# Attention and MoE on one core: seven products instead of eight for three quarters of the first pair's hidden layer

## Chip, core and metric

The kernel runs on one core of one Trainium2 chip. The metric is device time in microseconds (us), lower is better. Engines are named as the profile names them: PE (TensorE), PEld (its weight loads), ACT (ScalarE), DVE (VectorE), POOL (GpSimd) and SP (SyncE, which only issues transfers here).

## What is computed

Sigmoid attention over 8 batches, 12 heads, 448 positions and 64 channels, then a gated two-layer network over all 3584 tokens:

```
scores = q @ k^T / sqrt(64) - log(448)
attn   = sigmoid(scores)
x      = attn @ v              # heads side by side: 3584 x 768
h      = x @ w_in              # 3584 x 2048
g      = h * sigmoid(h)
out    = g @ w_out             # 3584 x 768
```

The kernel holds q, k, v and the weights as float16, accumulates in float32 and returns float32.

## The kernel before

The eight batches are taken in four pairs m = 0 to 3. For attention a *group* g is four heads of one batch (24 groups, three to a batch), and each group has seven *units* (g, ch), one per 64-row chunk of keys for two head pairs.

**Attention.** `scores` (L209) makes one unit: eight quarter-array products, four at a time, into one of two double PSUM banks (`psc`), then one ACT sigmoid of 128x896 (L223). Two units make a *burst* (`burst`, L722). `values` (L231) multiplies the seven units of a group with v: 28 quarter-array products into two banks `pav`, which DVE scales into `xT` (L256). Work of the second layer kind is put between the bursts so that PE has something to do while ACT makes sigmoids. PE takes its instructions strictly in the order of the program, and so do ACT and DVE; a helper of the language puts in the waits between engines.

**Hidden layer, pairs 1 to 3.** `h_pair` (L348) computes a pair's h with Strassen-Winograd's seven block products in place of eight: the tokens of the two batches are the block rows of x, the two halves of w_in's rows and columns are its blocks. For each of eight column groups i there are seven products `m1` to `m7` of three 128x128x448 matmuls each (21 in place of 24). They need four sums over w_in (`w_in_sums`, L308: tiles `SI1`, `SI2`, `SI4`, and one sum in place), made once for all pairs, and four sums over x (`x_sums`, L334: tiles `tx` 1, 2, 4, and one in place in `xT`), made per pair. The products are put together by five DVE additions of 128x448 per column group (`plus`, L374).

**Hidden layer, pair 0.** `first_h` (L537) uses no such sums: `h_unit(b, fc)` (L273) is six matmuls of 128x128x448 for one batch b and one of 16 column blocks fc, so 192 in all. For batch 0 the result is evicted by an ACT sigmoid into a room of the tag `tx` and a DVE multiplication (L291, L292), since ACT's loaded table is the sigmoid's while bursts run. For batch 1 ACT's Silu is used (L296). Four matmuls each of the first two units are issued early (`begin`, L676). Then batch 1's bursts (units n = 24, 26, ... 40) alternate with stretches of the stream: `stretch(stream, 1600)` (L712) takes matmuls, at 189 ns each, until 1600 ns are due, that is eight or nine. What is left of the 192, 99 matmuls, runs as one dense stretch after the bursts (L743). During this the sums over w_in (12 of 16 DVE instructions, the rest comes in the first out set) and over w_out (`w_sums`, L452: `T2`, `T3`, `T4` and one in place, 14 of 16, on DVE) are made, and `dma_transpose` (L198) prepares the k and q of groups 6, 7 and 8: a DVE copy of 128x896 (L202) and a transposing transfer by SP.

**Output layer.** `out_set` (L473) does two row blocks with seven products of eight 128x128x384 matmuls each, with the sums `T2` to `T4` over w_out and DVE sums over `gTr`. `sets` (L556) runs three or four of them per pair; after 14 matmuls of the first set the next pair's bursts are put among them.

**PSUM banks.** During bursts four single banks serve everything but `psc` (`one_bank`, L84). `banks_for_h` (L74) makes all eight single, in a ring that starts at the single bank that it takes for the oldest. A new tile in a bank waits until the old one's last reader is done.

```
    stream = first_h()
    stretch(stream, 1600)
    for n in range(NT_B + 3, 2 * NT_B, 2):
        burst(n)
        if n in (26, 30):
            transposes(5, "k" if n == 26 else "q")
        stretch(stream, 1600)
    values_if_any()
    for _ in stream:
        pass
```

Of the kernel before, what the change touches and what calls it, by code (L numbers as in the profile page):

```python
# [2 lines left out]

# [14 lines left out]
def kernel(  # L18
# [14 lines left out]
    P = 128  # L33
# [238 lines left out]

    def h_unit(b, fc):  # L273
        ph = one_bank("ph")
        for at, cc in enumerate(pairs):
            assert b in ready or at < 4
            nc.tensor.matmul(  # L277
                ph[:, :S],
                w_in_sb[:, cc, fc * P : (fc + 1) * P],
                xT[b][:, cc, :],  # L280
                start=(at == 0),
                stop=(at == NCC - 1),
            )
            if at < NCC - 1:
                yield 189
        if fc == NFC - 1:
            h_done.add(b)
        to = gTr[:, fc, first_col(0) + b * S : first_col(0) + (b + 1) * S]
        if b == 0:
            tsig = room_x()[:, 0]  # L290
            nc.scalar.activation(tsig, ph[:, :S], AF.Sigmoid, bias=0.0, scale=ISX)  # L291
            nc.vector.scalar_tensor_tensor(  # L292
                out=to, in0=ph[:, :S], scalar=ISX, in1=tsig, op0=ALU.mult, op1=ALU.mult
            )
        else:
            nc.scalar.activation(to, ph[:, :S], AF.Silu, bias=0.0, scale=ISX)  # L296
        yield 189


# [8 lines left out]
    def w_in_sums():  # L308
        for i in (1, 2, 4):
            si[i] = cpool.tile([P, NQ, NH], F16, tag=f"SI{i}", name=f"SI{i}")  # L310
        quarter = NH // 4

        def piece(at, op, o, x, y):
            cols = slice(at * quarter, (at + 1) * quarter)
            op(o[:, :, cols], x[:, :, cols], y[:, :, cols])

        add, sub = nc.vector.tensor_add, nc.vector.tensor_sub
        for half in range(2):
            for at in (2 * half, 2 * half + 1):
                piece(at, add, si[1], wi[1][0], wi[1][1])  # L320
                yield
            for at in (2 * half, 2 * half + 1):
                piece(at, sub, si[2], si[1], wi[0][0])
                yield
        for at in range(4):
            piece(at, sub, si[4], wi[0][1], si[2])
            yield
        for at in range(4):
            piece(at, sub, si[3], wi[0][0], wi[1][0])
            yield  # L330
# [3 lines left out]
    def x_sums(m, lo, hi):  # L334
        if lo == 0:
            for i in (1, 2, 4):
                tx[m, i] = room_x()
        of = slice(lo, hi)
        x0, x1 = ([xT[2 * m + j][:, c * NQ : (c + 1) * NQ] for c in range(2)] for j in range(2))
        sub = nc.vector.tensor_sub  # L340
        sub(tx[m, 1][:, of], x1[0][:, of], x0[0][:, of])
        sub(tx[m, 2][:, of], x1[1][:, of], tx[m, 1][:, of])
        sub(x1[0][:, of], x1[1][:, of], x1[0][:, of])
        sub(tx[m, 4][:, of], x0[1][:, of], tx[m, 2][:, of])

    NG = NFC // 2

    def h_pair(m, last_values):  # L348

        x0, x1 = xT[2 * m], xT[2 * m + 1]  # L350
# [11 lines left out]
        def product(i, to, w, x, start=True):  # L362
            for n in range(NQ):
                nc.tensor.matmul(  # L364
                    to,
                    w[:, n, i * P : (i + 1) * P],
                    x[:, n],
                    start=(start and n == 0),
                    skip_group_check=not start,
                    stop=(n == NQ - 1),  # L370
                )

# [25 lines left out]
        def m7(i):  # L398
            bank[i, "c"] = one_bank("pc")[:, :S]
            product(i, bank[i, "c"], si[3], x1[:, :NQ])  # L400
            got[i, "u3"], got[i, 22] = scratch(), scratch()
            plus(got[i, "u3"], bank[i, "c"], got[i, "u2"])
# [9 lines left out]
        def m3(i):  # L412
            product(i, bank[i, "d"], si[4], x1[:, NQ:], start=False)
            plus(bank[i, "d"], bank[i, "d"], got[i, "u2"])
            silu(i, 0, 1, bank[i, "d"])
# [3 lines left out]

        last = NG - 1  # L420
        order = [(m1, 0), (m1, 1), (last_values,), (m1, 2)]
        for i in range(3):
            order += [(m2, i), (silu11, i)]
        order += [(m5, 0), (m6, 0), (m7, 0), (h22, 0), (m1, 3)]
        for i in range(last):
            if i > 0:
                order += [(m7, i), (m5, i), (h22, i)]
            if 3 < i + 2 <= last:
                order += [(m1, i + 2)]
            order += [(silu22, i), (m6, i + 1)]  # L430
            if i < last - 1:
                order += [(m4, i), (m3, i)]
            if 2 < i + 2 < last:
                order += [(m2, i + 2), (silu11, i + 2)]
        order += [(m7, last), (m5, last), (h22, last), (m2, last), (silu11, last)]
        order += [(silu22, last), (m4, last - 1), (m3, last - 1), (m4, last), (m3, last)]
# [3 lines left out]
        h_done.update((2 * m, 2 * m + 1))  # L440

# [10 lines left out]
    def w_sums():  # L452
        for i in (2, 3, 4):
            tw[i] = cpool.tile([P, NHC, NO2], F16, tag=f"T{i}", name=f"T{i}")
        tw[1] = wq[0][1]
        for o, x, y in (
            (tw[3], wq[1][1], wq[0][1]),
            (tw[1], wq[0][1], wq[0][0]),
            (tw[2], wq[1][1], tw[1]),
            (tw[4], tw[2], wq[1][0]),  # L460
        ):
            for f in range(0, NHC, 2):
                nc.vector.tensor_sub(o[:, f : f + 2], x[:, f : f + 2], y[:, f : f + 2])
                yield
# [8 lines left out]
    def out_set(a1, rows1, a2, rows2, last=False):  # L473
# [13 lines left out]
        def product(a, w):  # L487
            po = one_bank("po")
            for fc in range(NHC):
                nc.tensor.matmul(  # L490
                    po[:, :NO2], a[:, fc, :], w[:, fc, :], start=(fc == 0), stop=(fc == NHC - 1)
                )
                if fc < NHC - 1:
                    yield 163
            return po[:, :NO2]
# [6 lines left out]
        yield 163  # L502
# [5 lines left out]
        yield 163  # L508
# [3 lines left out]
        yield 163  # L512
        po = yield from product(sg[2], tw[3])
        add(c22, po, c12)
        yield 163
        po = yield from product(a2[:, hi], tw[4])
        sub(c21, c22, po)
        yield 163
# [4 lines left out]
        yield 163  # L523
# [6 lines left out]
        yield 163  # L530

    by_h1 = {3: 6, 6: 7, 9: 8}
    early = [h_unit(0, fc) for fc in range(2)]
    sums = w_sums()
    in_sums = w_in_sums()

    def first_h():  # L537
        for b in range(2):
            for fc in range(NFC):
                yield from early[fc] if b == 0 and fc < 2 else h_unit(b, fc)  # L540
                if b == 0 and fc >= 10 or b == 1 and fc < 6:
                    next(in_sums)
                if b == 0:
                    continue
                if fc >= 2:
                    next(sums)
                if fc in by_h1:
                    for name in ("k", "q"):
                        dma_transpose(by_h1[fc], name, nc.vector.tensor_copy)
                    if by_h1[fc] == 8:  # L550

                        nc.gpsimd.tensor_copy(gate, qkT["q", 8][:1, 0, :1])
                        for to in (9, 10, 11):
                            load("kq", to)

    def sets(m):  # L556
        for g in range(0, NCH - 1, 2):
# [3 lines left out]
            for i, ns in enumerate(step):  # L561
                if m == 0 and g == 0 and i in (10, 14):
                    next(sums)
                if m == 0 and g == 0 and i in (20, 28, 36, 44):
                    next(in_sums)
                yield ns
# [62 lines left out]
    def after_values(g):  # L629
# [16 lines left out]
        if g >= 2 * NQ and g % (2 * NQ) == 2 * NQ - 2:  # L646
# [63 lines left out]
    done = due = 0.0  # L710

    def stretch(stream, ns, spent=0):  # L712
        nonlocal done, due
        due += ns
        done += spent
        while done < due:
            step_ns = next(stream, None)
            if step_ns is None:
                return
            done += step_ns  # L720

# [13 lines left out]
    stream = first_h()  # L735
    stretch(stream, 1600)
    for n in range(NT_B + 3, 2 * NT_B, 2):
# [3 lines left out]
        stretch(stream, 1600)  # L741
    values_if_any()
    for _ in stream:  # L743
        pass

    ENDING, FIRST_DENSE = 8, 14
    for m in range(B // 2 - 1):
        if m > 0:
            banks_for_attention()
# [20 lines left out]
        nc.scalar.activation(warm, bias_s, AF.Silu)  # L770
# [3 lines left out]
        waiting.clear()  # L774
        banks_for_h()
        values(g, NCH - 1)

        def last_values():
            values(g)
            after_values(g)  # L780
            x_sums(m + 1, NQ - 1, NQ)
            nc.gpsimd.tensor_copy(gate, tx[m + 1, 4][:1, NQ - 1, :1])

        for i, _ in enumerate(h_pair(m + 1, last_values)):
# [35 lines left out]
```

## Time and profile before

| what | value |
|---|---|
| median of 3 runs | 375.65 us (375.52 to 375.68) |
| the profiled execution's own time | 375.68 us |
| its span, first to last instruction | 373.7 us |
| granted TensorE clock over the span | 0.998 |
| PE busy | 363.9 us, 97% of the span |
| DVE, ACT, POOL busy | 252.2, 251.3, 77.4 us |

The first pair by stages, from the trace's timeline (us from the span's start):

| stage | from | to |
|---|---|---|
| start, batch 0's units up to 23 | 0 | 27.78 |
| first stretch, then batch 1's bursts n = 24 to 40 with 8 or 9 matmuls behind each | 27.78 | 55.58 |
| values of group 5 | 55.58 | 57.08 |
| dense stretch, 99 matmuls | 57.08 | 75.85 |
| out sets of pair 0 with the bursts of batches 2 and 3 begin | 75.85 | |

A row of the timeline is: start, time, engine, line, operation, output <- input, shapes, how many; in square brackets the idle time of the engine before it and what ended it. Times of several instructions in one row run from the first's start to the last's end; PE's rows overlap, because matmuls are pipelined and each one's shown duration (353 ns) is longer than the distance to the next.

### The profile page before, as it was taken

Reading aid. Unit: us, or ns where it says so; the run is one execution under the profiler, and the core shown is the slowest. Engines: PE = TensorE matmul, PEld = TensorE weight load, DVE = VectorE, ACT = ScalarE, POOL = GpSimd, SP = SyncE. Lnnn points to the kernel's source line nnn. Section 1 sums busy time; section 2 is a strip of 40 time slices with the busy share of each in tenths; the row PEclk is TensorE's granted clock in tenths of the full one; section 3 lists DMA queues with packets and bytes.
Section 4 is the critical chain, followed back from the end, with each engine's and each line's share of the span. In section 5 each row is a group of like instructions: output and inputs, shape, how many; then the busy total and the mean of one; then the engine's idle time right before and its main releaser. Section 6 shows DMA issues by size and latency. Waiting matters only on the chain.

```text
span 373.7 us, 7596 instructions
## 1 busy us (share of the span) xinstructions
PE 363.9 (97%) x3009; PEld 182.4 (49%) x3009; DVE 252.2 (67%) x458; ACT 251.3 (67%) x339; POOL 77.4 (21%) x116
## 2 busy tenths in 40 slices
PE   7999999999999999999999999999999999999995
PEld 3554445544444455544444545544444545555553
DVE  2565469867655687867575758795655768797763
ACT  5998885479888756687777846679888946650000
POOL 8566521040051072000014046000100000000000
PEclk9999999999999999999999999999999999999999
DMA  8999999996769599008579669921964030003333
GB/s 133 201 204 204 204 204 204 166 142 128 124 107 210 117 129 172 18 0 128 107 137 165 142 129 134 109 37 28 171 97 97 2 87 0 3 0 84 86 84 84
DMA packets 65698, 42.78 MB, mean 114 GB/s; under 512 B 36096, under 2 KB 62208, under 8 KB 65664
## 3 DMA queue, kind: packets, MB, share of 16 engines
q0 software_dynamic: 27072, 22.58, 42.3%
q1 hardware_dynamic: 38240, 19.44, 27.1%
q8 instruction: 23, 0.38, 0.4%
q10 hardware_dynamic: 352, 0.30, 0.2%
q14 instruction: 11, 0.09, 0.1%
HBM read 45.61 MB, written 11.01 MB: 152 GB/s over the span
## 4 chain that ended last, share of the span: by engine, by line
PE 79%; DMA 9%; ACT 6%; issue 2%; DVE 2%; POOL 0%; ACTq 0%
PE po L490 31%; PE psc L216 9%; PE pa L364 7%; PE pav L245 7%; PE pc L364 7%; PE pd L364 7%; ACT attnT L223 5%; PE ph L277 5%; DMA kf<-in_k_dram 5%; PE pb L364 4%; DMA qf<-in_q_dram 2%; DMA w_in_sb<-in_moe_w_in_dram 2%; PE pw L174 2%; ACT gTr L358 1%; PE ptrq L187 1%
## 5 line engine op out<-in xcount | busy, mean ns | idle before, releaser
L223 ACT ACTIVATE attnT<-psc,bias_s 128x896 f16<-128x896 f32 x168 | 159.2, 1009 | 25.9 <-PE psc L216 25.5
L490 PEld LDWEIGHTS <-S 128*128 128x128 f16 x448 | 40.8, 98 | 36.3 <-issue 10.0
L216 PE MATMUL psc<-qT,kT 64*64 64x448 f16 x672 | 54.8, 364 | 3.0 <-ACT attnT L223 1.8
L256 DVE TENSOR_SCALAR xT<-pav 128x448 f16<-128x448 f32 x48 | 27.7, 620 | 32.5 <-PE pav L245 32.5
L115 POOL DMA_DIRECT2D vf<-in_v_dram x24 | 17.2, 716 | 135.6 <-PE pav L245 131.4
L490 PEld LDWEIGHTS <-gTr 128*128 128x128 f16 x336 | 30.8, 98 | 27.7 <-issue 9.7
L490 PE MATMUL po<-w_out_sb,gTr 128*128 128x384 f16 x224 | 42.5, 327 | 0.1
L490 PE MATMUL po<-T,S 128*128 128x384 f16 x224 | 42.5, 327 | 0.0
L364 PEld LDWEIGHTS <-w_in_sb 128*128 128x128 f16 x288 | 27.7, 98 | 26.9 <-issue 1.7
L490 PE MATMUL po<-w_out_sb,S 128*128 128x384 f16 x224 | 40.4, 327 | 0.0
L245 PE MATMUL pav<-attnT,vf 64*64 64x448 f16 x672 | 39.1, 350 | 0.5 <-DVE gTr L292 0.4
L277 PE MATMUL ph<-xT,w_in_sb 128*128 128x448 f16 x192 | 38.7, 353 | 0.1
L216 PEld LDWEIGHTS <-kT 64*64 64x64 f16 x672 | 17.9, 104 | 35.8 <-issue 32.2
L364 PE MATMUL pa<-xT,w_in_sb 128*128 128x448 f16 x144 | 33.2, 353 | 0.0
L364 PEld LDWEIGHTS <-SI 128*128 128x128 f16 x216 | 21.1, 98 | 20.0 <-issue 0.5
L245 PEld LDWEIGHTS <-vf 64*64 64x64 f16 x672 | 21.8, 106 | 12.8 <-issue 4.7
L277 PEld LDWEIGHTS <-w_in_sb 128*128 128x128 f16 x192 | 17.8, 98 | 19.1 <-issue 3.7
L380 ACT ACTIVATE part<-pa 128x448 f32<-128x448 f32 x24 | 13.1, 544 | 20.1 <-PE pa L364 19.2
L490 PE MATMUL po<-T,gTr 128*128 128x384 f16 x112 | 22.2, 327 | 0.0
L358 ACT ACTIVATE gTr<-pc 128x448 f16<-128x448 f32 x24 | 13.1, 544 | 12.9 <-DVE pc L374 12.5
L374 DVE TENSOR_TENSOR part<-pb,part 128x448 f32<-128x448 f32 x24 | 14.9, 621 | 8.3 <-ACT part L380 5.0
L177 ACT ACTIVATE m<-po 128x384 f32<-128x384 f32 x1 | 0.5, 492 | 27.7 <-PE po L490 27.7
(76 smaller groups left out, 468.4 us busy)
## 6 DMA issues: line engine op xcount, KB each, us to landing
out_dram<-osb SPq DMA_DIRECT2D x54, 192.0 KB, 3.0
vf<-in_v_dram POOLq DMA_DIRECT2D x24, 224.0 KB, 6.7
kf<-in_k_dram POOLq DMA_DIRECT2D x23, 224.0 KB, 7.6
qf<-in_q_dram POOLq DMA_DIRECT2D x23, 224.0 KB, 8.1
w_in_sb<-in_moe_w_in_dram POOLq DMA_DIRECT2D x16, 192.0 KB, 8.1
w_out_sb<-in_moe_w_out_dram POOLq DMA_DIRECT2D x4, 768.0 KB, 14.8
kT<-kr SPq DMA_TRANSPOSE x18, 4.1
qT<-qr SPq DMA_TRANSPOSE x18, 4.4
```

The costliest lines, as they stand in the source:

```text
L115: nc.gpsimd.dma_start(flat[name, g][:, :, c0:c1].rearrange("p i c d -> p i (c d)"), rows_in(name, g)[:, :, c0 * D : c1 * D],)
L174: nc.tensor.matmul(pw, dummy[:, :P], dummy, start=True, stop=True)
L216: nc.tensor.matmul(psc[own, j, :S], qkT["k", g][rows, ch, own], qkT["q", g][rows, :, own], start=True, stop=True,)
L223: nc.scalar.activation(attnT[g, ch], psc[:, :, :S], AF.Sigmoid, bias=bias_s, scale=QKSCALE)
L245: nc.tensor.matmul(pav[half][j * D : (j + 1) * D, :S], flat["v", g][own, j, ch, :], at[own, j, :], start=(ch == 0), stop=(ch == NCH - 1),)
L256: nc.vector.tensor_scalar_mul(xT[b][:, half * NQ + iq, :], pav[half][:, :S], SX)
L277: nc.tensor.matmul(ph[:, :S], w_in_sb[:, cc, fc * P : (fc + 1) * P], xT[b][:, cc, :], start=(at == 0), stop=(at == NCC - 1),)
L358: nc.scalar.activation(gTr[:, r * NG + i, col + c * S : col + (c + 1) * S], h, AF.Silu, bias=0.0, scale=ISX)
L364: nc.tensor.matmul(to, w[:, n, i * P : (i + 1) * P], x[:, n], start=(start and n == 0), skip_group_check=not start, stop=(n == NQ - 1),)
L374: nc.vector.tensor_add(o, po, x)
L380: nc.scalar.activation(got[i, 1], bank[i, "a"], AF.Copy)
L490: nc.tensor.matmul(po[:, :NO2], a[:, fc, :], w[:, fc, :], start=(fc == 0), stop=(fc == NHC - 1))
```

## The change

Column groups 2 to 7 of pair 0's h (`PLAIN = 2` stay plain) are computed by the seven products too. Plain units remain for groups 0 and 1: 2 batches x 2 groups x 2 halves x 6 = 48 matmuls; the other six groups take 6 x 21 = 126.

- Among batch 1's bursts, where batch 1's x isn't there yet, `first_fill` runs what needs batch 0 alone: the four plain units of batch 0, and for groups 2 to 7 `early_m1` (three matmuls, then an ACT copy of the partial sum to SBUF, 128x448 float32, into rooms of the tags T2 and T4) and `early_m2` (three more into the same bank, then `to_sig`). A fixed number of matmuls stands behind each burst (`behind_burst`) in place of 1600 ns.
- `to_sig` takes its rooms from the tags S1 to S4, no longer from `tx`.
- `w_in_sums` goes quarter by quarter (1, 2, 3, then 0), four dependent instructions for each; 12 of the 16 are issued behind the bursts n = 32 to 40 (`sums_behind`), the last four in the second out set.
- `x_sums` is made for pair 0 too, with a tile of its own in place of the sum in `xT`.
- After the bursts `first_pair` takes the place of the dense stretch: values of group 5 (six rounds, four matmuls each of two units of batch 1, the seventh round, then the rest), and the products m5, m6, m7, m4, m3 of the six groups. It uses the eight-bank ring, so banks change before and after it.
- Sums over w_out: `T3` and `T2` by GpSimd (4 instructions of 128x768 each) during `first_pair`; `T2` is now `T3` plus a block, so that the sum in place may come last; `T4` and the sum in place by DVE in the first out set.
- The rows of groups 6, 7 and 8 are copied by ACT in place of DVE.

```diff
+    def to_sig(ph, to):
...
+        nc.scalar.activation(tsig, ph, AF.Sigmoid, bias=0.0, scale=ISX)
+        nc.vector.scalar_tensor_tensor(
+            out=to, in0=ph, scalar=ISX, in1=tsig, op0=ALU.mult, op1=ALU.mult
+        )
...
+        for at in (1, 2, 3, 0):
             cols = slice(at * quarter, (at + 1) * quarter)
+            for op, o, x, y in (
+                (add, si[1], wi[1][0], wi[1][1]),
+                (sub, si[2], si[1], wi[0][0]),
+                (sub, si[4], wi[0][1], si[2]),
+                (sub, si[3], wi[0][0], wi[1][0]),
+            ):
+                op(o[:, :, cols], x[:, :, cols], y[:, :, cols])
                 yield
...
+        def early_m1(i):
+            bank[i, "a"] = one_bank("pa")[:, :S]
+            yield from steps(i, bank[i, "a"], wi[0][0], x0[:, :NQ])
...
+            got[i, 1] = rooms["m1"].pop(0)
+            nc.scalar.activation(got[i, 1], bank[i, "a"], AF.Copy)
+            yield
+
+        def early_m2(i):
+            yield from steps(i, bank[i, "a"], wi[0][1], x0[:, NQ:], start=False)
+            to_sig(bank[i, "a"], gTr[:, i, col : col + S])
+            yield
...
+    def first_pair(p, last_values, rows, w_out_sums):
+        units = [h_unit(1, r * NG + i) for i in range(PLAIN) for r in range(2)]
+        last = NG - 1
+        order = [(starts, *units[:2]), (last_values,), (starts, *units[2:])]
+        order += [(ends, *units), (p.m5, PLAIN), (p.m6, PLAIN)]
+        for i in range(PLAIN, last):
+            order += [(p.m7, i)]
+            if i > PLAIN:
+                order += [(p.m5, i)]
+            order += [(p.h22, i), (p.silu22, i)]
+            if i > PLAIN:
+                order += [(rows,)]
+            order += [(p.m6, i + 1)]
+            if i < last - 1:
+                order += [(p.m4, i), (p.m3, i)]
+            if i > PLAIN:
+                order += [(rows,)]
+            if i == PLAIN + 1:
+                order += [(w_out_sums, 2)]
+        order += [(p.m7, last), (p.m5, last), (p.h22, last), (p.silu22, last)]
+        order += [(p.m4, last - 1), (p.m3, last - 1), (p.m4, last), (p.m3, last)]
...
+    def first_fill(p):
+        for unit in early:
+            yield from unit
+        yield from p.early_m1(PLAIN)
+        for i in range(PLAIN + 1, NG):
+            yield from p.early_m1(i)
+            yield from p.early_m2(i - 1)
+        yield from p.early_m2(NG - 1)
+        for i in range(PLAIN):
+            yield from h_unit(0, NG + i)
...
-        if g >= 2 * NQ and g % (2 * NQ) == 2 * NQ - 2:
+        if g % (2 * NQ) == 2 * NQ - 2:
             x_sums(g // (2 * NQ), 0, NQ - 1)
...
+    behind_burst = {24: 6, 26: 4, 28: 4, 30: 4, 32: 7, 34: 7, 36: 4, 38: 7, 40: 3}
+    sums_behind = {32: 2, 34: 2, 36: 3, 38: 3, 40: 2}
+    fill(stream, 6)
     for n in range(NT_B + 3, 2 * NT_B, 2):
         burst(n)
         if n in (26, 30):
             transposes(5, "k" if n == 26 else "q")
-        stretch(stream, 1600)
-    values_if_any()
-    for _ in stream:
-        pass
+        for _ in range(sums_behind.get(n, 0)):
+            next(in_sums)
+        fill(stream, behind_burst[n])
...
+    def last_part_of(g, m, then):
+        nc.scalar.activation(warm, bias_s, AF.Silu)
+        waiting.clear()
+        banks_for_h()
+        values(g, NCH - 1)
+
+        def last_values():
+            values(g)
+            after_values(g)
+            x_sums(m, NQ - 1, NQ)
+            nc.gpsimd.tensor_copy(gate, tx[m, 4][:1, NQ - 1, :1])
+            then()
+
+        return last_values
...
+    first_pair(first, last_part_of(g, 0, lambda: w_out_sums(3)), next_rows, w_out_sums)
```

228 lines of the change are left out of this document (114 added, 114 removed).

## The prediction

> **What bounds the kernel now.** First the page's busy times and the granted clock, then who made PE wait after the first pair, then PE's busy time by stage, then the timeline of the stage that changes.
>
> ```profile
> PE 363.9 (97%) x3009; PEld 182.4 (49%) x3009; DVE 252.2 (67%) x458; ACT 251.3 (67%) x339; POOL 77.4 (21%) x116
> ```
> ```profile
> PE psc L216 <- ACT attnT L223: 1.3, 8, 0.2
> ```
> ```profile
> 30.45:57.08 26.63, 25.82 (x262) 12.05 (x261) 14.50 (x27) 22.64 (x31) 11.75 (x16) 1.00 1.29 204
> 57.08:75.85 18.77, 18.71 (x103) 9.59 (x100) 16.01 (x33) 9.99 (x17) 2.72 (x5) 1.00 1.07 174
> ```
>
> PE is the bound nearly everywhere: 97% busy, clock 1.00 in both stretches (column behind POOL), and after 75 us it waits 1.3 us in all. In the dense stretch (second row) it does 99 matmuls in 18.77 us, 0.190 us each. In the bursts (first row) ACT is busy 22.64 of 26.63 us, second only to PE: if PE's work there shrinks by more than about 4 us, ACT becomes the bound. The timeline of the last bursts gives the steps:
>
> ```profile
> 51.15 0.57 PE L216 MATMUL psc<-qT,kT 64*64 64x448 f16 x8
> 51.58 1.91 ACT L223 ACTIVATE attnT<-psc,bias_s 128x896 f16<-128x896 f32 x2 [0.54 <-PE psc L216]
> ...
> 51.65 1.88 PE L277 MATMUL ph<-xT,w_in_sb 128*128 128x448 f16 x9
> 53.38 0.98 ACT L291 ACTIVATE tx<-ph 128x448 f16<-128x448 f32 x2
> 53.46 0.57 PE L216 MATMUL psc<-qT,kT 64*64 64x448 f16 x8
> ...
> 54.23 1.93 ACT L223 ACTIVATE attnT<-psc,bias_s 128x896 f16<-128x896 f32 x2
> ...
> 55.58 1.57 PE L245 MATMUL pav<-attnT,vf 64*64 64x448 f16 x28
> ```
>
> Two score sigmoids occupy ACT from 51.58 to 53.38, 0.90 us each; two evictions from 53.38 to 54.23, 0.43 each (a reader may go on 1.01 and 0.54 after their start). Scores cost PE 0.51 (51.15 to 51.65), nine matmuls and the switch back 1.81. DVE's steps are in pair 1's sums over x and in the sums over w_in:
>
> ```profile
> 119.62 1.16 DVE L256 TENSOR_SCALAR xT<-pav 128x448 f16<-128x448 f32 x2 [1.51 <-PE pav L245]
> 120.70 0.61 DVE L341 TENSOR_TENSOR tx<-xT 128x896 f16<-128x896 f16 x1
> 121.34 0.62 DVE L342 TENSOR_TENSOR tx<-xT,tx 128x896 f16<-128x896 f16 x1
> 121.89 0.62 DVE L343 TENSOR_TENSOR xT<-xT 128x896 f16<-128x896 f16 x1
> 122.42 0.62 DVE L344 TENSOR_TENSOR tx<-xT,tx 128x896 f16<-128x896 f16 x1
> 122.96 0.55 DVE L514 TENSOR_TENSOR osb<-po,osb 128x384 f32<-128x384 f32 x1
> ```
> ```profile
> 59.69 1.02 DVE L315 TENSOR_TENSOR SI<-SI,w_in_sb 128x768 f16<-128x768 f16 x2
> ```
>
> Two scalings and the four sums take 3.34 us (119.62 to 122.96). A sum over w_in takes 0.47 (1.02 less one duration of 0.55) behind an independent one; I take 0.57 behind the one whose result it reads (120.70 to 121.34 shows the result's 0.61 plus 0.03).
>
> **The change, part by part.** *Removed from PE:* 192 - 174 = 18 matmuls x 0.190 = 3.4 us. If nothing else changed, 372.2.
>
> *The split.* Before, 85 matmuls lie in the bursts and 99 behind. Now 52 lie in the bursts (6 + 46 by the table of counts) and 24 + 90 = 114 behind. So the dense part grows by 15 x 0.190 = 2.85 us, and the bursts must end 2.85 us earlier merely to break even. PE has 33 x 0.190 = 6.3 us less to do there. But ACT has as much as before: from unit 23's end on, 18 sigmoids and 16 evictions (6 copies and 10 sigmoids; before, 16 sigmoids, one behind the values). A product of three matmuls now gives an eviction, where six did before. ACT's floor: free at 29.32 (end of a run of 13 sigmoids), + 18 x 0.90 + 15 x 0.43 = 52.0 at best, and PE can't start the last round of values before.
>
> *The bursts laid out.* I put the changed program's instructions in their order on PE, ACT and DVE, with the steps above, and the waits that the built program has. Besides those: ACT starts 0.50 after a burst's first score matmul and 0.40 after an eviction's last matmul. Start of each burst's scores:
>
> | n | 24 | 26 | 28 | 30 | 32 | 34 | 36 | 38 | 40 |
> |---|---|---|---|---|---|---|---|---|---|
> | before | 30.45 | 32.58 | 36.10 | 39.54 | 42.37 | 44.49 | 46.88 | 51.15 | 53.46 |
> | after | 29.9 | 33.3 | 35.9 | 39.1 | 41.3 | 43.3 | 47.6 | 50.4 | 52.3 |
>
> The 6 us don't come off, for PE waits in line for ACT. Behind n = 24, m2 of group 2 may add to its bank only when ACT has copied m1, and that copy stands behind two score sigmoids: copied at 32.7, PE ready at 31.15, 1.6 us lost. Behind n = 34 it happens again with group 7: its copy stands behind units 34 and 35, done at 47.2, PE ready at 45.2, 2.0 lost. Banks whose tile is still read cost 0.7 (n = 26, transposed k), 0.35 and 0.3 (values of group 3, transposed q, both behind a `to_sig`), and double banks 0.25 and 0.5 (units 35 and 41). Together 5.7. Values of group 4 end at 49.5, as before. What of it is queued behind: all of PE.
>
> *DVE behind values of group 4.* From 49.4 DVE has, in this order: two scalings and four sums over x (3.34), three sums over w_in, group 7's multiplication, one sum, two sums, a multiplication, two sums, and last the multiplication of the last plain unit (`ph`, issued in n = 38 and 40). From the first sum over w_in to the start of that last multiplication are ten steps, three of 0.57 (each reads the sum just made) and seven of about 0.49 (0.47, or 0.54 behind an instruction of a scaling's kind), 5.1; its own duration is 0.62. So 49.4 + 3.3 + 5.1 + 0.6 = 58.4, and 58.5 with the handover. Before, there were no sums over x here and three over w_in ahead of the last values. PE now starts values of group 5 at 53.9, and the second of its two banks is the one that this last unit held: the built program has PE wait there for exactly that multiplication. So PE stands from 54.0 to 58.6, 4.6 us, and all that follows stands with it. ACT is through with unit 41 at 55.0 and would not hold it that long.
>
> *The dense part.* 22 of the 24 value matmuls 1.15; eight matmuls 1.6; the seventh round 0.4; 16 matmuls 3.1; m5, m6, m7 of group 2 and m6 of group 3, 12 matmuls, 2.3. m4 and m3 of group 2 wait for DVE (additions after m6 and m7) 0.5 in all. Then m4, m3 (1.1), three groups of 15 matmuls (2.84 each, 8.5) and 27 matmuls (5.1). 58.6 + 23.8 = 82.4: the out sets begin at 82.4 in place of 75.85, **+6.6**. Per group DVE has 5 additions, about 0.53 each back to back, 0.73 where one reads the last, under 2.84; pair 1's groups of 15 at 153.46 to 159.13 run without a PE wait. ACT has three evictions and two row copies per group in groups 3 to 5; nearest row: a score sigmoid of the same 896 columns at 0.90. 3 x 0.53 + 1.8 = 3.4 against 2.84, so it falls 1.7 behind and catches up in the last 27 matmuls (six evictions, 3.2 in 5.1); the banks that it holds aren't asked for until two groups later. If that cover were gone, the 0 to 1.7 would show. The copies taken from DVE would there have cost 6 x 0.5.
>
> *GpSimd's sums.* No two-input GpSimd instruction is in the trace. Nearest rows: its copy of 128x896, 0.94, thus 0.80 for 768 columns (low end); four times that, 3.2, as high end. I take 1.6, a pass for each input. `T3` can start at 64.5 (its gate needs the last sum over x), `T2` behind group 4's m6 at 71.3: done by 77.7, before the out set needs it at 86; hidden. At 3.2, `T2` is done at 90, and the third product waits some 3 to 4 us. [...]
>
> *The out sets.* DVE has 8 sums in the first set's first 34 steps where it had 6 in 44: 2 x 0.47 more, in a stage where DVE was busy 42.97 of 64.15 us: 0 to 0.5, I take 0. The loads of groups 9 to 11 are issued some 3 us later against the sets' start; their first row copy is 8.6 us after that start before, and the transfers' queue is empty by then: 0. The moved Silu load keeps its place among ACT's instructions: 0. SP has the same six transposes.
>
> Sum: -3.4 removed, +5.7 and +4.6 of new waits, -1.0 of waits in the old bursts that go, +0.5 in the dense part: +6.4; the layout gives **+6.6**. The profiled execution took 375.68 (span 373.7 and 2.0 around it), 0.03 over the median. So 380.3 of span, **382.2 us**.
>
> **The rivals.**
> *A: DVE's tail doesn't hold the bank* (it frees in time, or DVE is faster than its rows). Then values of group 5 end at 57.2, but their scaling is still queued behind the same sums (59.6), and the plain units' last matmuls wait for it: out sets at 78.5, +2.7, **378.4**. Against it: the wait is in the program and 17 instructions at 0.47 to 0.62 fill the time.
> *B, the other side: PE isn't held, the 18 matmuls come off.* It needs ACT's copies to come before the score sigmoids that they stand behind, and DVE to do its 17 instructions between the values of groups 4 and 5 in 4.5 us, 0.26 each, where no row of such size is under 0.38; it decides for faster only if the last values resume before 52.0, while unit 40's sigmoid ends at 54.1 here. **372.2**. For it: PE at 97% in every stretch shows that this kernel's waits were all hidden.
> *C: GpSimd's sums are slow* (3.2 each or held up by DVE): +3 to 4 more, **385.5**.
>
> **How the numbers follow.** Forecast 0.76, A 0.11, C 0.08, B 0.04, a draw between A and B 0.01. This kernel's measurement tells 0.2% (0.75 us) from no change. Faster 0.04, same 0.01, slower 0.95. The forecast's own range: bursts ±1.0 (how the copies fall between sigmoids), DVE's tail ±0.6, dense part -0.3 to +1.7: 380.4 to 384.6. Taking in A: **378.4 to 384.6**.
>
> **What would show it.** PE idle 4 to 5 us before `pav` of the fifth group, ended by a DVE multiplication into `gTr`; PE idle 1.6 and 2 us before `pa` matmuls, ended by ACT's copy to `m1s`; values of group 4 ending near 49.5; out sets beginning near 82.4; a PE stretch without waits from 69 to 82; GpSimd's sums of 1.6. Wrong, if `pav` starts before 56 without a wait, if the bursts n = 36 start before 46, or if PE waits in the out sets for `T2`.

## The result and the profile after

| | before | after |
|---|---|---|
| median | 375.62 us (4 runs, 375.52 to 375.68) | 386.53 us (4 runs, 385.26 to 387.63) |
| profiled execution, and its span | 375.68, 373.7 us | 387.63, 385.8 us |
| granted TensorE clock over the span | 0.998 | 0.987 |

The change makes the kernel slower: the ratio is 1.029, 95% interval 1.0247 to 1.0332, so 10.9 us where 6.6 were forecast. The direction was right, and the time lies 1.9 us above the upper end of the range. The four executions fall into two groups, 387.6 twice with a mean clock of 0.987, and 385.3 and 385.4 with 0.991; the profiled one is of the first.

First the page of the kernel after: the engines' busy times, and the granted clock in 40 slices.

```profile
PE 365.8 (95%) x2991; PEld 181.7 (47%) x2991; DVE 262.2 (68%) x476; ACT 258.4 (67%) x352; POOL 90.5 (23%) x125
...
PEclk9999986999999999999999999999999999999999
```

There are 18 fewer matmuls than before (2991 against 3009), and yet PE is busy 1.9 us longer. So some matmuls became longer, and the clock row says where: it leaves 9 in the sixth and seventh slice, 48 to 67 us. Just before this stretch, at 47.40, the longer of the two waits for ACT's copy ends, and the wait for DVE lies in it. The view of what PE waited for, over the whole span (total, times, longest):

```profile
PE pav L246 <- DVE gTr L287: 5.0, 2, 4.6
PE pa L368 <- ACT m1s L392: 3.4, 2, 1.9
...
PE po L558 <- ACT gTr L362: 1.4, 1, 1.4
```

The first two are the waits of the forecast (4.6; 1.6 and 2.0). The third was not in it. PE's timeline from the second wait for ACT's copy to the dense part:

```profile
47.40 0.35 PE L368 MATMUL pa<-xT,w_in_sb 128*128 128x448 f16 x1 [1.91 <-ACT m1s L392]
47.67 0.92 PE L217 MATMUL psc<-qT,kT 64*64 64x448 f16 x8
48.37 2.84 PE L246 MATMUL pav<-attnT,vf 64*64 64x448 f16 x28
...
55.44 0.38 PE L246 MATMUL pav<-attnT,vf 64*64 64x448 f16 x2
60.43 2.45 PE L246 MATMUL pav<-attnT,vf 64*64 64x448 f16 x22 [4.61 <-DVE gTr L287]
62.80 2.67 PE L295 MATMUL ph<-xT,w_in_sb 128*128 128x448 f16 x8
```

Before, 28 value matmuls took 1.57 (those of group 5, the line at 55.58 shown with the prediction). Here those of group 4 take 2.84: nothing waits inside, each matmul takes about twice as long. So are the 22 and the 8 behind the long wait (2.45 for 1.15 in the forecast's sum, 2.67 for 1.6). Now PE's busy time by stretches of 3.41 us, laid so that the changes of the clock fall on their borders; the columns are the stretch, its length, PE busy (matmuls), granted clock, DMA share, GB/s:

```profile
44.35:47.76 3.41, 1.50 (x11) 1.00 1.30 204
47.76:51.17 3.41, 3.41 (x37) 0.50 1.32 205
51.17:54.59 3.42, 3.28 (x31) 1.00 1.31 203
54.59:58.00 3.41, 1.23 (x9) 1.00 1.28 204
58.00:61.41 3.41, 0.98 (x12) 0.50 1.27 203
61.41:64.83 3.42, 3.42 (x20) 0.50 1.19 193
64.83:68.24 3.41, 3.41 (x22) 1.00 0.31 43
```

Each stretch in which PE had little to do (1.50, 1.23, 0.98 us) is followed by one at a granted clock of 0.50. So a wait costs twice here: once itself, and once more in the work behind it. Before, the clock was 1.00 from 47 to 76 us.

What DVE and GpSimd do agrees with the forecast. From DVE's timeline, the first and the last steps between the two values, and from GpSimd's, the sums over w_out:

```profile
51.24 1.16 DVE L257 TENSOR_SCALAR xT<-pav 128x448 f16<-128x448 f32 x2 [2.81 <-PE pav L246]
52.31 0.62 DVE L347 TENSOR_TENSOR tx<-xT 128x896 f16<-128x896 f16 x1
...
58.29 0.62 DVE L287 SCALAR_TENSOR_TENSOR gTr<-ph,sig 128x448 f16<-128x448 f32 x1
...
59.76 0.62 DVE L287 SCALAR_TENSOR_TENSOR gTr<-ph,sig 128x448 f16<-128x448 f32 x1
```
```profile
68.52 6.44 POOL L531 TENSOR_TENSOR T<-w_out_sb 128x768 f16<-128x768 f16 x4
75.70 6.45 POOL L531 TENSOR_TENSOR T<-T,w_out_sb 128x768 f16<-128x768 f16 x4 [0.74 <-ACT gTr L362]
```

DVE works without a gap from 51.24 to 60.38, 9.1 us, and PE goes on at 60.43. Four sums by GpSimd take 6.44, 1.61 each, and the second set ends at 82.15, ahead of the out sets. These begin late, and pair 1's begin with a wait; PE's timeline at the two places:

```profile
86.38 2.44 PE L558 MATMUL po<-w_out_sb,gTr 128*128 128x384 f16 x14
...
171.47 2.44 PE L558 MATMUL po<-w_out_sb,gTr 128*128 128x384 f16 x14 [1.37 <-ACT gTr L362]
```

The span grew by 12.1 us. Out sets of pair 0 begin at 86.38; before, the same line stands at 76.04 (the table of stages and the prediction have 75.85, where only its weights are loaded; from matmul to matmul the layout's +6.6 is +6.4). The forecast's 82.4 accounts for 6.4 of these 10.3 us, half the clock for 4.0, as the experiments below show. Pair 1's wait is 1.4, and 0.4 is spread over the rest.

### The profile page after: what moved, and what is told of

The parts are those of the page before. It is cut to its first block, busy times and chain, and to the rows that moved or that the text cites. A ratio compares the mean times of both kernels' runs of the same rounds, so it can differ in the third digit from the quotient of the medians.

```text
span 385.8 us, 7628 instructions
## 1 busy us (share of the span) xinstructions
PE 365.8 (95%) x2991; PEld 181.7 (47%) x2991; DVE 262.2 (68%) x476; ACT 258.4 (67%) x352; POOL 90.5 (23%) x125
## 4 chain that ended last, share of the span: by engine, by line
PE 81%; ACT 10%; DVE 5%; issue 3%; ACTq 0%; DVEq 0%
PE po L558 30%; PE psc L217 9%; PE pav L246 9%; PE pc L368 8%; PE pd L368 8%; PE pa L368 8%; ACT attnT L224 7%; PE pb L368 4%; PE ph L295 2%; ACT gTr L362 2%; PE pw L175 1%; DVE SI L331 1%; DVE gTr L287 1%; DVE xT L257 1%; DVE kT L195 1%
## 5 line engine op out<-in xcount | busy, mean ns | idle before, releaser
L368 PEld LDWEIGHTS <-w_in_sb 128*128 128x128 f16 x360 | 34.1, 98 | 36.8 <-issue 6.4
L246 PE MATMUL pav<-attnT,vf 64*64 64x448 f16 x672 | 42.0, 367 | 5.1 <-DVE gTr L287 5.0
L368 PE MATMUL pa<-xT,w_in_sb 128*128 128x448 f16 x180 | 41.9, 353 | 3.7 <-ACT m1s L392 3.4
L368 PEld LDWEIGHTS <-SI 128*128 128x128 f16 x270 | 26.4, 98 | 25.1 <-issue 0.7
L246 PEld LDWEIGHTS <-vf 64*64 64x64 f16 x672 | 22.6, 111 | 19.2 <-issue 11.2
L368 PE MATMUL pc<-tx,w_in_sb 128*128 128x448 f16 x108 | 26.3, 352 | 0.3 <-DVE part L401 0.3
L362 ACT ACTIVATE gTr<-pc 128x448 f16<-128x448 f32 x30 | 16.3, 543 | 13.3 <-DVE pc L401 12.8
L362 ACT ACTIVATE gTr<-part 128x448 f16<-128x448 f32 x30 | 17.2, 575 | 9.6 <-DVE part L401 9.6
L401 DVE TENSOR_TENSOR part<-pc,part 128x448 f32<-128x448 f32 x30 | 18.6, 622 | 6.3 <-PE pc L368 5.5
L368 PE MATMUL pb<-tx,SI 128*128 128x448 f16 x90 | 21.9, 352 | 0.0
```

Source lines behind the costliest of these rows:

```text
L246: nc.tensor.matmul(pav[half][j * D : (j + 1) * D, :S], flat["v", g][own, j, ch, :], at[own, j, :], start=(ch == 0), stop=(ch == NCH - 1),)
L362: nc.scalar.activation(gTr[:, r * NG + i, col + c * S : col + (c + 1) * S], h, AF.Silu, bias=0.0, scale=ISX)
L368: nc.tensor.matmul(to, w[:, n, i * P : (i + 1) * P], x[:, n], start=(start and n == 0), skip_group_check=not start, stop=(n == NQ - 1),)
L401: nc.vector.tensor_add(o, po, x)
```

## The experiments

The theory: the layout of the forecast holds, and two things are missing in it, the clock behind PE's waits and a bank that pair 1's first output product shares with the last product before it. The rivals: the extra time is in the bursts (ACT or DVE slower than their rows), or in the bank alone. All kernels are the changed one with the edit named; the ratio is to the kernel before on the same chip.

| run | edit | median us (range) | ratio, 95% interval |
|---|---|---|---|
| clock_fill | PE kept busy in two waits | 383.22 (383.07–383.29) | 1.0208, 1.0191–1.0225 |
| ring0 | another bank for group 5's values | 381.6 (381.16–383.17) | 1.0171, 1.0148–1.0194 |
| sums_last | 8 sums over w_in behind the plain units | 382.69 (382.22–384.49) | 1.0202, 1.0176–1.0228 |
| dve_copies | copies of m1 by DVE | 385.5 (384.79–386.74) | 1.0271, 1.0248–1.0294 |
| ring1 | other banks in pair 1 | 385.82 (385.38–385.91) | 1.0271, 1.0254–1.0288 |
| table | m2 one burst later | 384.37 (383.18–384.94) | 1.0232, 1.0211–1.0252 |
| combo | table, sums, ring1 | 380.81 (379.18–381.07) | 1.0132, 1.0109–1.0155 |
| combo_e | combo, ring0 | 377.54 (377.31–377.75) | 1.0054, 1.0039–1.0069 |
| combo_f | combo_e, three copies by DVE | 376.62 (376.24–376.69) | 1.0025, 1.0014–1.0035 |
| combo_g | combo_e, six copies by DVE | 376.84 (376.2–377.09) | 1.0029, 1.0017–1.0040 |
| combo_h | combo_f, banks of pair 1 again | 375.44 (374.9–375.7) | 1.0000, 0.9992–1.0009 |
| combo_i | combo_h, a fourth copy by DVE | 376.04 (375.62–376.52) | 1.0013, 1.0005–1.0022 |

### Keep PE busy where it waits (clock_fill)

```diff
         def early_m2(i):
+            if i == NG - 1:
+                keep_busy(9)
...
         pav, done_rounds = part_of.pop(g, None) or (
...
+        if g == 5 and done_rounds == 0:
+            for _ in range(20):
+                nc.tensor.matmul(pav[0], dummy[:, :P], dummy, start=True, stop=True)
```

> The changed kernel with 9 dummy matmuls (128x128x512) put where PE waits for group 7's copy of m1, and 20 in the first bank of the fifth group's values, where PE waits 4.6 us for DVE; the waits themselves stay. Theory (PE's own idleness halves its granted clock, for 3.2 us from 48 and 6.8 us from 58): the clock is 1.00 from 45 to 70, values of group 4 take 1.5 us and not 2.8, the out sets begin near 82.5 and not 86.3; time 3 to 4 us under the changed kernel's, 382.5 to 383.5. Rival (the matmuls are slow there for another reason, such as the transfers at 204 GB/s or two readers of one memory): the slow stretches stay, 386 to 388.

Measured 383.22, inside the theory's range: 3.3 us less than the changed kernel, with 29 matmuls more. PE's timeline in this kernel:

```profile
47.95 1.49 PE L249 MATMUL pav<-attnT,vf 64*64 64x448 f16 x28
...
53.58 4.48 PE L243 MATMUL pav<-dummy 128*128 128x512 f16 x20
57.99 1.33 PE L249 MATMUL pav<-attnT,vf 64*64 64x448 f16 x24
```

The 28 value matmuls are back at 1.49, and the granted clock is 1.000 over the span. From the values to the out sets (81.85) it is 23.9 us, where the forecast had 23.8 and the changed kernel needs 25.95. One thing limits the reading. The nine matmuls take a bank of their own, which turns the ring by one: the program no longer makes group 5's values wait for the last plain unit, and here it is the 20 added matmuls that fill the place of the wait and end 0.6 us ahead of where the forecast had the bank free (58.6). With these 0.6 the out sets would stand at 82.4, as forecast. DVE's own timeline agrees. With group 4's values at full clock, the last multiplication of its tail ends at 58.61:

```profile
58.00 0.61 DVE L290 SCALAR_TENSOR_TENSOR gTr<-ph,sig 128x448 f16<-128x448 f32 x1
```

So in the changed kernel's trace the clock costs 86.38 - 82.4 = 4.0: values resume at 60.43 instead of 58.6, since DVE's tail starts 1.84 later behind the slow values of group 4 (51.24, where the forecast had 49.4), and 2.1 more are lost behind (25.95 less 23.8).

### Give group 5's values another bank (ring0)

```diff
+    SINGLES_FIRST = {0: [5, 7, 6, 4]}
...
         ring[:] = [2 * NDOUBLE + (oldest + i) % NSINGLE for i in range(NSINGLE)]
+        ring[:] = SINGLES_FIRST.get(m, ring)
```

> The changed kernel with another order of the four single banks for pair 0's ring (5, 7, 6, 4 in place of 7, 4, 5, 6): the fifth group's values take the banks of group 7 and of the fourth group's values, and the bank of the last plain unit is taken two tiles later. Theory (bank and DVE's queue together): values begin at 56.9 in place of 60.4, when group 7's multiplication is done, but the plain units behind them wait for two later multiplications (58.9 and 60.4) in the same queue: 1.9 us come off, and 0 to 2.2 more of clock: 382.4 to 384.6. Rival (the bank alone): the whole wait of 4.6 goes and the clock's loss with it, 379 to 381. Rival (the wait is for something else): no change, 386.5.

Measured 381.6, 0.8 under the theory's range and above the first rival's. PE's waits in this kernel's timeline:

```profile
47.04 0.35 PE L371 MATMUL pa<-xT,w_in_sb 128*128 128x448 f16 x1 [1.91 <-ACT m1s L395]
54.91 1.33 PE L249 MATMUL pav<-attnT,vf 64*64 64x448 f16 x24 [1.39 <-DVE gTr L290]
56.97 0.92 PE L298 MATMUL ph<-xT,w_in_sb 128*128 128x448 f16 x4 [0.73 <-DVE gTr L290]
58.44 0.92 PE L298 MATMUL ph<-xT,w_in_sb 128*128 128x448 f16 x4 [0.55 <-DVE gTr L290]
```

In place of the 4.61 there are 1.39, 0.73 and 0.55, together 2.67: part of the wait moved to the units behind. The clock stays at 1.00 in this profile, although the wait of 1.91 ahead of 47.04 is there as in the changed kernel. One of the four executions has 0.993, and it took 383.17.

### Take sums out of DVE's tail (sums_last)

```diff
-    sums_behind = {32: 2, 34: 2, 36: 3, 38: 3, 40: 2}
+    sums_behind = {32: 2, 34: 2}
...
     assert next(stream, 0) == 0
+    for _ in range(8):
+        next(in_sums)
```

> The changed kernel with the eight sums over w_in of bursts 36 to 40 issued on DVE behind the last plain unit's multiplication; nothing is left out. Theory (DVE's queue holds the bank): the multiplication is done as soon as ACT's sigmoid is, near 57.7, the values resume 2.7 us earlier, the sums are hidden behind values and plain units: 383.8, or down to 381.5 if PE's shorter idle time keeps the clock. Rival (the sums only move the delay to the scaling of the fifth group's values behind them): under 1 us, 385.5 to 387.

Measured 382.69. The wait for the bank falls from 4.61 to 1.96 us in the profile: the sums held it for 2.65. What is left is ACT's: in this trace DVE stands idle for 1.38 us before the last multiplication, at 55.23, until ACT's sigmoid of the same unit is done. Half the clock lasts 3.41 us here (56.91 to 60.32) where it lasted 6.83, and the stretch behind the wait for ACT's copy is missing.

### Take the copies from ACT (dve_copies)

```diff
-            nc.scalar.activation(got[i, 1], bank[i, "a"], AF.Copy)
+            nc.vector.tensor_copy(got[i, 1], bank[i, "a"])
```

> The changed kernel with the six copies of m1 by DVE in place of ACT. Theory (the copies stand behind two score sigmoids on ACT): PE's waits of 1.45 and 1.9 us before m2 go, burst 36 begins at 44.3 to 45 in place of 47.7, the clock's first drop goes, values of group 4 end 4 us earlier, and DVE's tail with them (its 9 us stay): 381.5 to 383. Rival (DVE has no room for 6 x 0.53 us more and the tail ends no earlier): 385.5 to 388.

Measured 385.5, at the lower edge of the rival's range; but the rival's reason, that the tail ends no earlier, is not what the trace shows. The waits, and DVE's timeline before the last of them:

```profile
PE pav L246 <- DVE gTr L287: 5.0, 2, 4.6
PE pa L368 <- DVE m1s L392: 2.2, 3, 1.3
```
```profile
44.75 0.55 DVE L331 TENSOR_TENSOR SI<-w_in_sb,SI 128x768 f16<-128x768 f16 x1
45.22 0.55 DVE L331 TENSOR_TENSOR w_in_sb<-w_in_sb 128x768 f16<-128x768 f16 x1
45.68 0.61 DVE L392 COPY m1s<-pa 128x448 f32<-128x448 f32 x1
```

The copy no longer stands behind two score sigmoids, but behind two sums over w_in: 3.4 us of waits for ACT became 2.2 for DVE. The burst n = 36 starts at 46.63, 1.0 earlier than in the changed kernel (the theory had 3 earlier), and DVE's tail makes PE wait 4.61 as before, up to 57.74. In this profile the first stretch at half the clock is absent (mean clock 0.990), as it is in that of ring1 below, where values resume at 58.76; so the tail ends 1.0 earlier here. At like mean clocks the executions took 384.8 and 385.1 where the changed kernel took 385.3 and 385.4, and 385.9 and 386.7 where it took 387.6: 0.4 less in the one pair, 1.3 in the other.

### The other bank (ring1)

```diff
+    SINGLES_FIRST = {1: [6, 7, 4, 5]}
```

> The changed kernel with the single banks of pair 1's products in the order 6, 7, 4, 5, as the kernel before has them, instead of 7, 4, 5, 6; nothing else is different. Theory (the 1.37 us before pair 1's output products stands because their first bank is the one that the last product of pair 1 has just filled): that wait goes and the time falls by 1.4 us against the changed kernel (386.5 to about 385.1). Rival (the output products wait there for ScalarE's last results whatever bank they take): the wait stays under another name and the time is unchanged within 0.3 us.

The wait of 1.37 at pair 1's first output product is gone, but the median fell by 0.7 only, and the two executions of the changed kernel with the same mean clock (0.991) took 385.3 and 385.4, no more than this one. PE's waits hold the reason:

```profile
PE pav L249 <- DVE osb L596: 0.6, 1, 0.6
```

With this order the first values of pair 1 take the bank that DVE has just been adding into `osb`. From pair 0's out sets to pair 1's it is 84.28 us, against 85.09 in the changed kernel: of 1.37, some 0.6 are paid at another place. The cause of the wait is confirmed, the gain not.

### The product one burst later (table)

```diff
-    behind_burst = {24: 6, 26: 4, 28: 4, 30: 4, 32: 7, 34: 7, 36: 4, 38: 7, 40: 3}
+    behind_burst = {24: 4, 26: 6, 28: 4, 30: 4, 32: 7, 34: 6, 36: 5, 38: 7, 40: 3}
```

> The changed kernel with the second product of a group, which needs the scaled copy that ScalarE makes behind a burst, set behind the next burst in three places (7 products less... 6, 5 behind bursts 24 to 36 as: 24:4, 26:6, 34:6, 36:5 for 24:6, 26:4, 34:7, 36:4). Theory (the two waits of 1.45 and 1.91 us are a product that comes too early for its copy, and the second of them brings the first stretch at half the clock, some 1.3 us): both waits go, the clock is 1.00 until the wait for the bank at the end of the values, the time is 3 to 5 us below the changed kernel (381.5 to 383.5). Rival (the bursts are bound by ScalarE and the products only wait elsewhere; VectorE's tail then still ends as late): the waits show up at another product, the stretch to the output products shortens by less than 1.5 us, 385 to 386.5.

Measured 384.37, between the two. Both waits for ACT's copy are gone, and the clock is 1.00 up to 56.26; the values of group 5 resume at 56.71 instead of 60.43 (0.5 of this is an earlier start of the program: the burst n = 24 begins at 29.39 here and at 29.88 in the changed kernel). But scores now wait for ACT, and the long wait stays:

```profile
PE pav L246 <- DVE gTr L287: 5.0, 2, 4.4
PE psc L217 <- ACT attnT L224: 3.4, 12, 0.6
```

In the changed kernel scores waited 1.8 for ACT. Nearly half of what the products no longer wait comes back there: ACT has the same work in the bursts as before, which is the forecast's argument for its floor.

### All of it together (combo to combo_i)

combo has table's order, ring1's banks, and four of the twelve sums over w_in behind the last plain unit (the others earlier: `sums_behind = {32: 4, 34: 4}`). combo_e adds ring0's banks, combo_f and combo_g give DVE the copies:

```diff
+    SINGLES_FIRST = {0: [5, 7, 6, 4], 1: [6, 7, 4, 5]}
...
+            if i < 5:
+                nc.vector.tensor_copy(got[i, 1], bank[i, "a"])
+            else:
                 nc.scalar.activation(got[i, 1], bank[i, "a"], AF.Copy)
```

In combo_g the condition is `i < 8`. combo_h is combo_f with `1: [7, 5, 4, 6]`; combo_i has `if i < 5 or i == NG - 1`.

> The changed kernel with three edits at once: the products set as in the run named table, four of the twelve sums over the input weights moved behind the last group of VectorE's work (the others earlier), and pair 1's banks as in ring1. Theory (waits of 1.45, 1.91 and 1.37 us, two stretches at half the clock worth 3.9 us, and the wait of 4.61 us shortened by four sums of 0.6 us): 376 to 379.5, clock 1.00 throughout. Rival (part of the seven products' gain is taken by VectorE whatever the order, so the wait for the bank stays at 4 us and the clock drops behind it): 380 to 383.

> As combo, and the bank of group 5's values is one that was read earlier (single banks of pair 0 in the order 5, 7, 6, 4 instead of 7, 4, 5, 6), so that no values wait for VectorE's last plain result. Theory: the wait for the bank goes too, and what is left of it stands at the following products that take their sums from VectorE: 375 to 378, 1 us under combo, about the kernel before. Rival (VectorE is the bound of the whole stretch, and PE waits the same sum a few us later): as combo within 0.5 us.

> As combo_e, with the first three of the six copies behind the bursts (groups 2, 3 and 4) made by VectorE instead of ScalarE. Theory (with the order mended, what is left of the loss is ScalarE, busy from 39.9 to 54.1 us without a gap in combo_e; a copy taken from it gives back its 0.43 us): bursts end 1.3 us earlier, 376.2 to 376.8. Rival (VectorE's multiplications into gTr and the banks behind them come later by as much): 377.3 or more.

> As combo_e, with all six copies behind the bursts made by VectorE. Theory as for combo_f: 2.6 us off ScalarE, 375.0 to 376.2, level with the kernel before (375.6) or 0.6 us below. Rival (VectorE, with 3.2 us more ahead of the scaling of group 5's values, holds the plain units and the first sums over x instead): 377 to 380, waits of PE for VectorE's xT or tx between 56 and 64 us.

> As combo_f, with the single banks of pair 1's products in the order 7, 5, 4, 6 in place of 6, 7, 4, 5: neither the first values (with 6 first, they take the bank of the last output product of pair 0, and PE waited 0.65 us for VectorE's osb at 126.7 in combo_f) nor the first output product of pair 1 (with 7, 4, 5, 6, the 1.37 us of the changed kernel) takes a bank just used. Theory: 0.65 us off, 375.9 to 376.2, so level with the kernel before within 0.2%. Rival (ScalarE or VectorE behind it take the 0.65 back): 376.4 to 376.8.

> As combo_h, with the copy of the last group (7) by VectorE too. Theory (ScalarE sets the pace of the scores up to the copy of group 7 at 45.2 us, and VectorE has room there): 0.4 us more, 375.5 to 375.8. Rival (the score units that PE waits for stand ahead of that copy, so nothing is gained, and VectorE's later work is 0.5 us later): 375.9 to 376.4.

combo came 1.3 us above the theory's range, at the edge of the rival's (380.81). The wait for the bank is 1.96 in its profile, so not the rival's 4; its one execution at a clock of 1.00 took 379.18, the three at 0.995 took 380.8 to 381.1. combo_e is as the theory said: without that wait, 377.54 and clock 0.999 or 1.00 in all its executions. combo_f gave 0.9 of the 1.3 expected for three copies of 0.43, inside the theory's range; the other three, in combo_g, gave nothing more (376.84, between the ranges of theory and rival): PE now waits 1.0 for DVE's copies where it waited 1.4 more for ACT.

combo_h is level with the kernel before, within 0.1%, and 0.5 under its theory's range. Its out sets start at 75.91 (before 76.04, combo_f 76.30), but 0.4 of the distance to combo_f is there before the first burst of batch 1 (n = 24 at 29.46 and 29.87). The two programs differ in the banks of pair 1 alone. The matmuls that open the program, on a dummy tile, took 3.70 us in combo_h's profile and 4.02 in those of combo_f, combo_i, the changed kernel and the kernel before; first combo_h, then combo_i:

```profile
1.46 3.70 PE L178 MATMUL pw<-dummy 128*128 128x512 f16 x9 [1.46 <-DVE bias_s L677]
```
```profile
1.46 4.02 PE L178 MATMUL pw<-dummy 128*128 128x512 f16 x9 [1.46 <-DVE bias_s L677]
```

So an absolute time in one of these profiles compares with that of another to about 0.5 us only. What PE waits for from 26 to 80 us in combo_h is:

```profile
PE psc L220 <- ACT attnT L227: 1.6, 3, 0.6
PE pc L371 <- DVE part L407: 0.3, 1, 0.3
PE ptrq L191 <- DVE gTr L290: 0.2, 1, 0.2
PE po L564 <- ACT gTr L365: 0.2, 1, 0.2
```

The 0.65 us at pair 1's values are gone: out set to out set takes 83.24 against 83.95 in combo_f. PE is busy 361.1 us in this kernel, 362.3 in combo_f and 363.9 before, while combo_h's span is only 0.2 less than before. The saving of the seven products has become idle time of PE: in 29.4 to 75.9 us, PE is idle 3.0 us, where the two stretches of before that the prediction shows (30.45 to 75.85) hold 0.9. No run beat the kernel before.

combo_i gained nothing, as its rival said: its waits from 26 to 80 us are those of combo_h, so the fourth copy freed nothing. Of the 0.6 by which its median lies above combo_h's, the profiles have 0.4 at 29.88 (combo_h 29.46), ahead of all that the two programs do differently, and the same 0.4 still at the out sets (76.33). It goes with the 4.02 in place of 3.70 at the start. Whether the executions without a trace differ there too, no run tells.

## Why the prediction was wrong where it was

**What held.** The bursts: PE started their scores at

| n | 24 | 26 | 28 | 30 | 32 | 34 | 36 | 38 | 40 |
|---|---|---|---|---|---|---|---|---|---|
| forecast | 29.9 | 33.3 | 35.9 | 39.1 | 41.3 | 43.3 | 47.6 | 50.4 | 52.3 |
| measured | 29.88 | 33.23 | 35.60 | 39.12 | 41.41 | 43.34 | 47.67 | 52.00 | 53.94 |

To n = 36 it is right to 0.3 us. The waits for ACT's copies are 1.45 and 1.91 (forecast 1.6 and 2.0), the smaller ones 0.33, 0.43 and 0.23 (forecast 0.7, 0.35 and 0.3). DVE's tail is 9.1 us long (49.4 to 58.5 in the forecast), ends with the multiplication that the forecast named, and PE waits 4.61 for it (4.6). The dense part from 68.76 to the out sets has no wait above 0.3. GpSimd's sums are 1.61 (1.6), hidden. So rival A falls (the bank was held), and so do B and C; none of the signs that the prediction named for being wrong came up. ring0 did A's experiment: without the bank the time is 381.6, not 378.4, since the units behind wait for the same DVE, and the wait at pair 1's first output product is in it as well (1.4 in its profile).

**The step that failed** is "Values of group 4 end at 49.5, as before", and with it "So PE stands from 54.0 to 58.6, 4.6 us, and all that follows stands with it", then "58.6 + 23.8 = 82.4". Each of these takes the matmuls behind a wait at the duration that they have in the trace of before. But that trace has hardly a wait in these stages, and its clock is 1.00 there. Values of group 4 end at 51.14, and behind the long wait the clock is 0.50 up to 64.83. That is 4.0 us in the profiled execution. In two of the other three it is less: at a mean clock of 0.987 half the clock lasts 2 x 0.013 x 385.8 = 10.0 us (3.41 + 6.83 in the trace), at 0.991 6.9. The pairs of executions differ by 2.2 us, so the first of the two stretches is probably worth about that, and by the mean clocks it occurred in two of four; only one execution of this kernel has a trace. The range had no term for it: its ±1.0 for the bursts and ±0.6 for DVE are about when the work starts, none about how fast it runs. Its upper end is also under the sum of its own terms: 382.2 + 1.0 + 0.6 + 1.7 is 385.5, not 384.6; the measured 386.5 lies above both.

**A second step was missing.** "So 380.3 of span" leaves all behind the start of the out sets as before. The 1.37 us at 171 us are a bank: the extra tiles of the first pair shift the order in which pair 1's products take banks, and the first output product gets the one of the last product. ring1 shows that as the cause; by that edit 0.8 of it goes from the trace, and nothing of it shows in the time at a like mean clock. combo_h has an order without either wait.

**The size.** Forecast 382.2; plus 4.0 for the clock and 1.4 for the bank is 387.6, and the profiled execution took 387.63. That the sum meets the last digit is chance: from matmul to matmul the layout is 6.4 and not 6.6, 0.4 of the longer span has no place in it, and the term of -1.0 for waits of the old bursts is 0.8 in the trace of before (0.37 and 0.44). The median, 386.5, mixes both pairs of executions. Without the clock's part the kernel would be at 383.2 to 383.6 (clock_fill; 387.6 less 4.0), inside the forecast's own range though the 1.4 for the bank is in it.

## What to carry to other kernels

When a forecast puts waits of the size seen here (1.9 and 4.6 us) on TensorE, price the work behind them too: a wait of 1.9 us cost some 2 more where the clock fell and nothing more where it did not, and one of 4.6 another 2.1. Covering the two waits with idle matmuls was worth 3.3 us here although what stands in their place is only 0.6 shorter, shortening the wait of 4.6 by 2.65 was worth 3.8, and breaking it up 4.9. And an edit that takes more or fewer buffers from a ring moves every later user of the ring: look at which buffer the first instruction of each later stage gets.

## What the runs showed of the hardware

In the changed kernel's profile the granted clock changes at 47.76, 51.17, 58.00 and 64.83 us, that is one, two and two steps of 3.41 apart. In five profiles the half-clock stretches last 3.41 us (47.76 to 51.17 here; table 56.26 to 59.67; sums_last 56.91 to 60.32) or 6.83 (58.00 to 64.83 here; ring1 57.46 to 64.29; dve_copies 54.43 to 61.26), one or two of the same unit. In the stretch of 3.41 us just ahead, PE was busy 1.50 and 1.23 us where the clock fell here, 0.98 where it had fallen and stayed at 0.50 for one more stretch, 1.45 in sums_last and 0.00 in table (52.85 to 56.26). In ring1's profile one with 1.62 was followed by a clock of 1.00, and one with 0.09 by 0.50:

```profile
43.81:47.22 3.41, 1.62 (x10) 1.00 1.31 205
47.22:50.63 3.41, 3.27 (x49) 1.00 1.31 204
...
54.05:57.46 3.41, 0.09 (x2) 1.00 1.30 204
57.46:60.87 3.41, 2.11 (x22) 0.50 1.26 204
```

So in these profiles, with one exception, half the clock followed the stretches at full clock with 1.50 us of work or less and did not follow those with 1.62 or more. The wait of 1.9 us is followed by half the clock in the changed kernel's profile and not in ring0's and ring1's, and by the mean clocks not in half of the changed kernel's executions. That this depends on how the wait falls between the steps of 3.41 is my estimate from the 1.50 of the changed kernel and the 1.62 of ring1. The exception is in dve_copies: one with 1.98 was followed by half the clock and another with 1.98 was not:

```profile
44.19:47.60 3.41, 1.98 (x24) 1.00 1.30 203
47.60:51.02 3.42, 3.42 (x39) 1.00 1.31 202
51.02:54.43 3.41, 1.98 (x15) 1.00 1.31 203
54.43:57.84 3.41, 0.10 (x4) 0.50 1.29 205
```

So what exactly lowers the clock is not shown by the runs. In ring1's last row PE is busy 2.11 us at 0.50, and the next stretch (60.87 to 64.29) is at 0.50 again; that work at half the clock counts for less would be a guess from this one row.
